# First head's keys loaded in pairs, an elementwise maximum of score tiles, and that head's softmax placed after the next head's first key tile, in a decode kernel of cached attention and a gated MLP

## The chip, the cores and the metric

The kernel runs on one core of one Trainium2 chip. The metric is device microseconds of one execution. The median of three runs is given, and one more execution is profiled.

## The reference

One token goes through two branches, which a scalar gate mixes. Cut to what matters:

```python
g = sigmoid((x * gate_w).sum(-1, keepdims=True))
# branch A: 32 query heads share 4 key/value heads, 65536 cached positions, 128 wide
q = (x @ wq).reshape(1, 1, 32, 128).transpose(0, 2, 1, 3)
k = repeat(k_cache, 8, axis=1);  v = repeat(v_cache, 8, axis=1)
p = softmax(einsum('bhqd,bhkd->bhqk', q, k) * 128 ** -0.5, axis=-1)
a = einsum('bhqk,bhkd->bhqd', p, v).reshape(1, 1, 4096) @ wo
# branch B: gelu(x @ w_in), its second half normalised, scaled by w_sp and
# shifted by b_sp, times its first half, then @ w_out
out = g * a + (1 - g) * b
```

All inputs are bfloat16. The caches of keys and of values are 64 MB each (4 heads of 16 MB), and with the weights about 162 MB are read.

## The kernel before, in words

**Tiles.** The cache of one key/value head (G = 4 heads) is cut into NT = 4 tiles of 4 MB. Partition p of a tile holds 128 consecutive positions of 128 bf16, 32 KB. `load_kv` (L189) loads one tile, or two neighbouring ones as one DMA of 8 MB, in which each partition's row is 64 KB. All loads, the weights too, go into one buffer `kv` with NKV = 5 places of 4 MB. The argument `at` says at which place a load begins. A load is issued by SyncE (L184, the queue SP), in program order, and first waits until whatever last read those places is done. Only the two results and some small vectors take another queue.

**A key tile**, `k_tile` (L398). In four steps of a quarter tile each, VectorE transposes in place (L403), and TensorE multiplies the result with the query matrix `wt` (L410, 8 matmuls per step), all of it accumulating into the PSUM tile `s_ps` (two buffers, tag "s"). ScalarE then copies it to a bf16 tile `sc` of 128 x 1024 (L421). The maximum of `sc` along the row is written to one column of `mx` by a reduction (L405); it is kept in the list `late` and issued in the next key tile, behind that tile's first transpose.

**A head's softmax**, `stats` (L424). It issues the reduction that is left (L425), reduces the four columns to one (`m1`, L427), and takes the maximum over the partitions by a transpose on TensorE (`mt_ps`, L429), a small reduction (`gm`), a copy (`gr`), a small matmul (`nb_ps`, L436) and a scaling (`nb`, L439). Then for each of the four tiles ScalarE computes the exponential with its sum (L443) and VectorE transposes the result into `pt` (L446). The first exponential is preceded by a load of ScalarE's function table.

**A value tile**, `v_tile` (L449), is 32 matmuls with `pt` as weights (L456), accumulating a head's four tiles in `o_ps`. `head_out` (L464) turns them into the head's part of the output vector, and `build_w` (L386) makes the query matrix `wt` of a head on VectorE. `project` (L503) multiplies a vector with rows of an output weight.

**The order.** Every engine executes in program order (a dependency between each two instructions of an engine is added at the end). The program first loads w_in to places 3 to 4.75 and wq to places 0 to 2, and computes branch B's vector and the queries. Head 0's keys follow as four loads of one tile each, to places 2, 3, 0 and 1, each followed by its `k_tile`. Then w_out is loaded to place 4 and projected, and `stats(0)` runs. For each further head g, in two halves h: a pair of its keys is loaded to places 2 and 3 (h = 0) or 3 and 4 (h = 1), the tile in place 3 is processed first and then the other, a pair of the values of head g-1 is loaded to places 0 and 1, and its two tiles are processed; in the second half `stats(g)` stands between the two value tiles. After the loop come the last head's values, wo and the output.

Of the kernel before, what the change touches and what calls it, by code (L numbers as in the profile page):

```python
# [8 lines left out]
FP32 = mybir.dt.float32  # L9
BF16 = mybir.dt.bfloat16  # L10
I32 = mybir.dt.int32
ACT = mybir.ActivationFunctionType
ALU = mybir.AluOpType
AX = mybir.AxisListType

P = 128
CT = 128
NKV = 5
B = 32
NB = P // B  # L20
VC = 4
CC = CT // VC
# [7 lines left out]
def kernel(  # L30
# [15 lines left out]
    nc = tc.nc  # L46
# [12 lines left out]
    NT = S // (P * CT)  # L59
# [9 lines left out]
    wk = ctx.enter_context(tc.tile_pool(name="wk", bufs=2))  # L69
    big = ctx.enter_context(tc.tile_pool(name="big", bufs=1))  # L70
# [9 lines left out]
    def same_weights(ins):  # L80
        held.add(ins.ins.name)
# [95 lines left out]
    def load(src, shape, at):  # L177
        n = 1
        for s in shape:
            n *= s  # L180
        v = kv[:, int(at * CT * P):int(at * CT * P) + n]
        if len(shape) == 2:
            v = v.rearrange("p (a b) -> p a b", b=shape[1])
        ins = nc.sync.dma_start(out=v, in_=src)  # L184
        if not first_load:
            first_load.append(ins.ins.name)
        return v

    def load_kv(src, g, j, at, n=1):  # L189
        h, i = divmod(j, 2)  # L190
        rows = src[0, g, 2 * h * CT * P:2 * (h + 1) * CT * P, :].rearrange(
            "(p c) d -> p (c d)", c=2 * CT)
        v = load(rows[:, i * CT * DH:(i + n) * CT * DH], (n * CT * DH,), at)
        return [v[:, i * CT * DH:(i + 1) * CT * DH] for i in range(n)]
# [60 lines left out]
    for t in range(2):  # L255
        nc.vector.tensor_tensor(  # L256
            out=xm[:, t], in0=xb_ps[:, t * P:(t + 1) * P].rearrange("p (i c) -> p c i", c=KC),
            in1=sel_i[:].unsqueeze(1).to_broadcast([P, KC, P // KC]), op=ALU.mult)
# [51 lines left out]
    for hf in range(2):  # L310
        nc.vector.tensor_tensor(
            out=zm[:, hf], in0=z_ps[:, hf * HN:hf * HN + ZN].rearrange("p (j c) -> p j c", c=FC),
            in1=own_b[:].unsqueeze(2).to_broadcast([P, B, FC]), op=ALU.mult)
    z = wk.tile([P, 2 * FC], FP32, name="z")
    nc.vector.tensor_reduce(out=z[:].rearrange("p (h c) -> p h c", h=2),
                            in_=zm.rearrange("p h j c -> p h c j"), axis=AX.X, op=ALU.add)
# [24 lines left out]
                            op=ALU.subtract)  # L341
# [19 lines left out]
    for k in range(NHB):  # L361
        xs = slice(k * NX // NHB, (k + 1) * NX // NHB)
        nc.vector.tensor_tensor(  # L363
            out=qm[:, xs], in0=q_ps[:, k * HN:(k + 1) * HN].rearrange("p (x j e) -> p x j e",
                                                                   j=B, e=2),
            in1=own_b[:].unsqueeze(1).unsqueeze(3).to_broadcast([P, NX // NHB, B, 2]), op=ALU.mult)
    q1 = wk.tile([P, NX, 2], FP32, name="q1")
    nc.vector.tensor_reduce(out=q1[:], in_=qm.rearrange("p x j e -> p x e j"), axis=AX.X,
                            op=ALU.add)
    q4 = wk.tile([P, NB, NX * 2], BF16, name="q4")  # L370
    nc.vector.tensor_tensor(
        out=q4[:], in0=q1[:].rearrange("p x e -> p (x e)").unsqueeze(1).to_broadcast(
            [P, NB, NX * 2]),
        in1=own_n[:].unsqueeze(2).to_broadcast([P, NB, NX * 2]), op=ALU.mult)
# [6 lines left out]
    for g in range(G):  # L381
        k, t0 = g * T2 // NB, g * T2 % NB
        nc.vector.tensor_copy(out=qs[:, g].rearrange("p b (t h) -> p b t h", t=T2),
                              in_=qv[:, k, t0:t0 + T2].rearrange("p t h b -> p b t h"))

    def build_w(g):  # L386
        for v in range(VC):
            nc.vector.tensor_tensor(
                out=wt[g % 2][:, v, :, :, v, :],
                in0=qs[:, g].unsqueeze(2).to_broadcast([P, BP, NB, REP]),  # L390
                in1=own_n[:].unsqueeze(1).unsqueeze(3).to_broadcast([P, BP, NB, REP]),
                op=ALU.mult)

    oa = const.tile([P, OC], BF16, name="oa")
    late = []
    sct, ptt, mxs, lss, o_ps = {}, {}, {}, {}, {}

    def k_tile(g, j, kn):  # L398
        kb = kn.bitcast(I32)
        n = CC * DH // 2  # L400
        s_ps = pss.tile([P, 2 * HN], FP32, name="s_ps", tag="s")
        for v in range(VC):
            nc.vector.transpose(out=kb[:, v * n:(v + 1) * n], in_=kb[:, v * n:(v + 1) * n])  # L403
            while late:
                nc.vector.reduce_max(**late.pop())  # L405
            kx = kn[:, v * CC * DH:(v + 1) * CC * DH].rearrange(
                "p (c h k e) -> p h e c k", h=2, k=B, e=2)
            for b in range(BP):
                for k in range(2):
                    ins = nc.tensor.matmul(  # L410
                        s_ps[:, k * HN:(k + 1) * HN],
                        lhsT=wt[g % 2][:, v, b].rearrange("p a v h -> p (a v h)"),
                        rhs=kx[:, b // 2, b % 2, k * CC // 2:(k + 1) * CC // 2, :],
                        start=(v == 0 and b == 0), stop=(v == VC - 1 and b == BP - 1),
                        skip_group_check=True)
                    if k > 0:
                        same_weights(ins)
        if g not in mxs:
            mxs[g] = wk.tile([P, NT], FP32, name="mx")
        sct[g, j] = scp.tile([P, CC * B], BF16, name="sc")  # L420
        nc.scalar.copy(out=sct[g, j][:], in_=s_ps[:])  # L421
        late.append(dict(out=mxs[g][:, j:j + 1], in_=sct[g, j][:], axis=AX.X))

    def stats(g):  # L424
        nc.vector.reduce_max(**late.pop())  # L425
        m1 = wk.tile([P, 1], FP32, name="m1")
        nc.vector.reduce_max(out=m1[:], in_=mxs[g][:], axis=AX.X)  # L427
        mt_ps = psm.tile([1, P], FP32, name="mt_ps", tag="m")
        nc.tensor.transpose(mt_ps[:], m1[:], ident_f[:])  # L429
        gm = wk.tile([1, REP], FP32, name="gm")  # L430
        nc.vector.tensor_reduce(out=gm[:], in_=mt_ps[:].rearrange("p (a h) -> p h a", h=REP),
                                axis=AX.X, op=ALU.max)
        gr = wk.tile([1, P // REP, REP], FP32, name="gr")
        nc.vector.tensor_copy(out=gr[:], in_=gm[:].unsqueeze(1).to_broadcast([1, P // REP, REP]))
        nb_ps = psm.tile([P, 1], FP32, name="nb_ps", tag="m")
        nc.tensor.matmul(nb_ps[:], lhsT=gr[:].rearrange("p a h -> p (a h)"),  # L436
                         rhs=ones_f[0:1, 0:1], start=True, stop=True)
        nb = wk.tile([P, 1], FP32, name="nb")
        nc.vector.tensor_scalar(out=nb[:], in0=nb_ps[:], scalar1=-SCALE, scalar2=None,  # L439
                                op0=ALU.mult)  # L440
        lss[g] = wk.tile([P, NT], FP32, name="ls")
        for j in range(NT):
            nc.scalar.activation(out=sct[g, j][:], in_=sct[g, j][:], func=ACT.Exp, scale=SCALE,  # L443
                                 bias=nb[:, 0:1], accum_out=lss[g][:, j:j + 1])
            ptt[g, j] = ptp.tile([P, CC, B], BF16, name="pt")
            nc.vector.transpose(out=ptt[g, j][:].rearrange("p c x -> p (c x)"),  # L446
                                in_=sct[g, j][:])
# [55 lines left out]
    def project(w, n, vec, c0, first=False, last=False):  # L503
        for c in range(n):
            for t in range(NB):
                nc.tensor.matmul(  # L506
                    out_ps[t * B:(t + 1) * B, :],
                    lhsT=vec[:, c0 + c:c0 + c + 1].to_broadcast([P, B]),
                    rhs=w[:, c, t * NO:(t + 1) * NO],
                    start=(first and c == 0), stop=(last and c == n - 1),  # L510
                    skip_group_check=True)


    build_w(0)
    for j, n, at in ((0, 1, 2), (1, 1, 3), (2, 1, 0), (3, 1, 1)):
        for i, kn in enumerate(load_kv(A_k_cache, 0, j, at, n)):
            k_tile(0, j + i, kn)
        if j == 1:
            build_w(1)
    project(load(B_w_out.rearrange("(p c) n -> p c n", c=FC), (FC, D), 4), FC, uT, 0, first=True)  # L520
    stats(0)
    for g in range(1, G):
        for h in range(2):
            kn = load_kv(A_k_cache, g, 2 * h, 2 + h, 2)
            for i in ((1, 0), (0, 1))[h]:
                k_tile(g, 2 * h + i, kn[i])
            if h == 0 and g + 1 < G:
                build_w(g + 1)
            vn = load_kv(A_v_cache, g - 1, 2 * h, 0, 2)
            v_tile(g - 1, 2 * h, vn[0])  # L530
            if h == 1:
                stats(g)
            v_tile(g - 1, 2 * h + 1, vn[1])
        head_out(g - 1)
# [61 lines left out]
```

## Time and profile before

| | |
|---|---|
| median of 3 runs | 382.27 us (382.05 to 382.38) |
| the profiled execution | 382.16 us, its span 380.7 us |
| busy | PE 233.2 us (61%), PEld 56.0 (15%), DVE 218.5 (57%), ACT 39.6 (10%), POOL 4.4 (1%) |
| DMA | 162.17 MB, mean 426 GB/s over the span |
| key transposes (L403) | 64, mean 2281 ns |
| score matmuls (L410) | 512, busy 141.8 us |
| value matmuls (L456) | 512, busy 61.7 us |
| maxima (L405, L425) | 16 reductions, mean 1210 and 1220 ns |
| exponentials (L443) | 16, mean 1137 ns |

PE is TensorE, PEld its weight loads, DVE VectorE, ACT ScalarE, POOL GpSimd and SP SyncE. Times in views are microseconds from the start of the span. A letter q behind an engine means its instruction queue. In a timeline a line holds the start, the length, the engine, the line of the kernel, the operation, the tile written and the tiles read, the shapes, the count, and in brackets the idle time of the engine before it and what ended that. The slices of the page cut the span into 40 equal parts; a digit is the busy share in tenths, 9 standing for 90% or more. The chain of waits follows the work that ended last back to what released it.

### The profile page before, as it was taken

How to read it: one execution, taken by the hardware profiler on the slowest of the kernel's cores; microseconds unless marked ns; L12 is line 12 of the kernel's file. 1: busy time of each engine (PE TensorE's matmuls, PEld its weight loads, DVE VectorE, ACT ScalarE, POOL GpSimd, SP SyncE). 2: the span in 40 equal slices, each digit the busy share in tenths (PEclk: the TensorE clock that was granted, in tenths of full speed). 3: DMA queues.
4: the chain of work that ended last, by engine and by line, in shares of the span. 5: the costliest groups of instructions: out<-in, count | busy, mean ns of one | idle time of the engine just before them, and what ended most of it. 6: DMA issues, size and time to landing. Idle time of an engine off the chain costs nothing.

```text
span 380.7 us, 2605 instructions
## 1 busy us (share of the span) xinstructions
PE 233.2 (61%) x1395; PEld 56.0 (15%) x800; DVE 218.5 (57%) x211; ACT 39.6 (10%) x55; POOL 4.4 (1%) x10
## 2 busy tenths in 40 slices
PE   0060657876157944796397729871977196839386
PEld 0010101111101210111011101120211011202113
DVE  4133288997597506966977059669970388460040
ACT  1001001110601100114010001050100000500000
POOL 4000000000000000000000000000000000000000
PEclk9995769899759895989688958895989579969789
DMA  9998999999999999999999999999999999999995
GB/s 386 496 420 379 411 438 441 437 483 430 387 420 441 441 436 441 427 441 441 434 436 441 441 427 434 406 423 441 434 434 429 420 441 442 436 410 430 424 443 223
DMA packets 3943, 162.17 MB, mean 426 GB/s; under 512 B 472, under 2 KB 476, under 8 KB 860
## 3 DMA queue, kind: packets, MB, share of 16 engines
q1 hardware_dynamic: 3892, 162.01, 98.8%
q8 instruction: 8, 0.13, 0.1%
q14 instruction: 3, 0.02, 0.0%
q10 hardware_dynamic: 40, 0.01, 0.0%
HBM read 162.01 MB, written 0.00 MB: 426 GB/s over the span
## 4 chain that ended last, share of the span: by engine, by line
DMA 57%; PE 26%; DVE 13%; ACT 2%; issue 1%; SPq 1%; DVEq 0%; ACTq 0%
DMA kv<-in_A_k_cache_dram 43%; PE s_ps L410 21%; DMA kv<-in_A_wo_dram 7%; DVE kv L403 7%; DMA kv<-in_A_v_cache_dram 7%; PE o_ps L456 4%; DVE pt L446 2%; DVE o_sb L470 1%; DVE mx L405 1%; ACT sc L421 1%; ACT sc L443 1%; DVE rowt L466 1%; SPq L184 1%; PE om_ps L476 0%; DVE osum L486 0%
## 5 line engine op out<-in xcount | busy, mean ns | idle before, releaser
L410 PE MATMUL s_ps<-kv,wt 128*128 128x512 bf16 x512 | 141.8, 437 | 80.2 <-DVE kv L403 80.2
L403 DVE STREAM_TRANSPOSE kv<-kv 128x2048 int32<-128x2048 int32 x64 | 142.7, 2281 | 54.3 <-DMA kv<-in_A_k_cache_dram 54.3
L456 PE MATMUL o_ps<-kv,pt 128*64 128x512 bf16 x512 | 61.7, 400 | 7.6 <-DMA kv<-in_A_v_cache_dram 7.6
L410 PEld LDWEIGHTS <-wt 128*128 128x128 bf16 x256 | 27.6, 108 | 195.6 <-issue 138.5
L421 ACT CAST sc<-s_ps 128x1024 bf16<-128x1024 f32 x16 | 16.2, 1012 | 249.9 <-PE s_ps L410 249.9
L456 PEld LDWEIGHTS <-pt 128*64 128x64 bf16 x256 | 16.1, 115 | 50.6 <-issue 48.1
L446 DVE STREAM_TRANSPOSE pt<-sc 128x1024 bf16<-128x1024 bf16 x16 | 18.6, 1217 | 6.8 <-ACT sc L443 6.8
L405 DVE TENSOR_REDUCE mx<-sc 128x1 f32<-128x1024 bf16 x12 | 14.5, 1210 | 9.9 <-ACT sc L421 9.9
L443 ACT ACTIVATE sc<-sc,nb 128x1024 bf16<-128x1024 bf16 x16 | 18.2, 1137 | 12.3 <-DVE nb L439 12.2
L466 DVE TENSOR_TENSOR rowt<-o_ps,own 128x1024 f32<-128x1024 f32 x4 | 4.8, 1195 | 24.9 <-PE o_ps L456 24.9
L476 PE MATMUL om_ps<-o_sb,hsel 128*32 128x128 f32 x8 | 2.3, 386 | 18.3 <-DVE o_sb L470 18.3
L425 DVE TENSOR_REDUCE mx<-sc 128x1 f32<-128x1024 bf16 x4 | 4.9, 1220 | 13.6 <-ACT sc L421 13.6
L296 PE MATMUL q_ps<-kv,xT 128*32 128x512 bf16 x64 | 5.6, 527 | 7.2 <-DMA kv<-in_A_wq_dram 7.2
L252 PE MATMUL xb_ps<-xg,spread 8*128 8x256 bf16 x1 | 0.4, 366 | 13.2 <-DMA xg<-in_gate_w_dram 13.2
L470 DVE TENSOR_REDUCE o_sb<-rowt 128x128 f32<-128x1024 f32 x4 | 7.5, 1872 | 0.1
L363 DVE TENSOR_TENSOR rowt<-q_ps,own_b 128x512 f32<-128x512 f32 x2 | 1.3, 686 | 10.8 <-PE q_ps L296 10.8
L296 PE MATMUL z_ps<-kv,xT 128*32 128x448 bf16 x64 | 5.9, 560 | 0.0
L495 PE MATMUL busy_ps<-wt 128*128 128x512 bf16 x23 | 5.8, 381 | 0.1
L506 PE MATMUL out_ps<-kv,oa 128*32 128x256 bf16 x128 | 4.2, 274 | 2.0 <-DMA kv<-in_A_wo_dram 2.0
L256 DVE TENSOR_TENSOR xm<-xb_ps,sel_i 128x128 f32<-128x128 f32 x2 | 0.5, 287 | 8.0 <-PE xb_ps L252 8.0
L552 ACT CAST out_sb<-out_ps 128x256 bf16<-128x256 f32 x1 | 0.4, 372 | 45.1 <-PE out_ps L506 45.1
L296 PEld LDWEIGHTS <-xT 128*32 128x32 bf16 x64 | 2.6, 136 | 14.6 <-issue 14.6
(90 smaller groups left out, 59.3 us busy)
## 6 DMA issues: line engine op xcount, KB each, us to landing
kv<-in_A_k_cache_dram SPq DMA_DIRECT2D x4, 4096.0 KB, 35.4
kv<-in_A_v_cache_dram SPq DMA_DIRECT2D x2, 4096.0 KB, 26.0
kv<-in_B_w_in_dram SPq DMA_DIRECT2D x1, 7168.0 KB, 19.4
kv<-in_A_wo_dram SPq DMA_DIRECT2D x1, 6144.0 KB
kv<-in_B_w_out_dram SPq DMA_DIRECT2D x1, 3584.0 KB
kv<-in_A_wo_dram SPq DMA_DIRECT2D x1, 1024.0 KB
kv<-in_A_wo_dram SPq DMA_DIRECT2D x1, 512.0 KB
kv<-in_A_wo_dram SPq DMA_DIRECT2D x2, 256.0 KB, 28.2
```

The lines of the kernel that those rows point to most:

```text
L296: ins = nc.tensor.matmul(ps[t * B:(t + 1) * B, k * HN:k * HN + n], lhsT=xT[:, i * KH + c:i * KH + c + 1].to_broadcast([P, B]), rhs=w[:, c, ...
L403: nc.vector.transpose(out=kb[:, v * n:(v + 1) * n], in_=kb[:, v * n:(v + 1) * n])
L405: nc.vector.reduce_max(**late.pop())
L410: ins = nc.tensor.matmul(s_ps[:, k * HN:(k + 1) * HN], lhsT=wt[g % 2][:, v, b].rearrange("p a v h -> p (a v h)"), rhs=kx[:, b // 2, b % 2, ...
L421: nc.scalar.copy(out=sct[g, j][:], in_=s_ps[:])
L425: nc.vector.reduce_max(**late.pop())
L443: nc.scalar.activation(out=sct[g, j][:], in_=sct[g, j][:], func=ACT.Exp, scale=SCALE, bias=nb[:, 0:1], accum_out=lss[g][:, j:j + 1])
L446: nc.vector.transpose(out=ptt[g, j][:].rearrange("p c x -> p (c x)"), in_=sct[g, j][:])
L456: ins = nc.tensor.matmul(o_ps[g][hs, e, :], lhsT=ptt[g, j][:, 2 * u:2 * u + 2, :].rearrange("p c x -> p (c x)"), rhs=vx[:, 2 * u + e], sta ...
L466: nc.vector.tensor_tensor(out=om8, in0=o_ps[g][:].rearrange("p e (v d) -> p (e v) d", d=DH), in1=own_8[:].unsqueeze(2).to_broadcast([P, 2 ...
L470: nc.vector.tensor_reduce(out=o_sb[:], in_=om8.rearrange("p x d -> p d x"), axis=AX.X, op=ALU.add)
L495: ins = nc.tensor.matmul(ps[:, :HN], lhsT=w[:, :P], rhs=w[:, :HN], start=True, stop=True, skip_group_check=True)
```

## The change

Three things change. Head 0's keys are loaded as two pairs, tiles 0 and 1 to places 2 and 3 and tiles 2 and 3 to places 0 and 1, instead of four single tiles; `build_w(1)` stays behind the second tile. The maximum of a head's scores is no longer taken by a reduction per tile: the first `sc` tile is kept as it is, each later one is joined by an elementwise maximum over 128 x 1024 into one bf16 tile `mx`, and `stats` reduces that tile once along its rows. And `stats(0)` is called after the first key tile of head 1 instead of before it. The other heads' `stats` stay where they are.

```diff
+    mx = big.tile([P, CC * B], BF16, name="mx")
+
+    def running_max(g, sc):
+        if g in mxs:
+            nc.vector.tensor_tensor(out=mx[:], in0=mxs[g][:], in1=sc[:], op=ALU.max)
+            mxs[g] = mx
+        else:
+            mxs[g] = sc
+
     def k_tile(g, j, kn):
...
             while late:
-                nc.vector.reduce_max(**late.pop())
+                running_max(*late.pop())
...
-        if g not in mxs:
-            mxs[g] = wk.tile([P, NT], FP32, name="mx")
         sct[g, j] = scp.tile([P, CC * B], BF16, name="sc")
         nc.scalar.copy(out=sct[g, j][:], in_=s_ps[:])
-        late.append(dict(out=mxs[g][:, j:j + 1], in_=sct[g, j][:], axis=AX.X))
+        late.append((g, sct[g, j]))
 
     def stats(g):
-        nc.vector.reduce_max(**late.pop())
+        while late:
+            running_max(*late.pop())
         m1 = wk.tile([P, 1], FP32, name="m1")
         nc.vector.reduce_max(out=m1[:], in_=mxs[g][:], axis=AX.X)
...
     build_w(0)
-    for j, n, at in ((0, 1, 2), (1, 1, 3), (2, 1, 0), (3, 1, 1)):
-        for i, kn in enumerate(load_kv(A_k_cache, 0, j, at, n)):
+    for j, at in ((0, 2), (2, 0)):
+        for i, kn in enumerate(load_kv(A_k_cache, 0, j, at, 2)):
             k_tile(0, j + i, kn)
-        if j == 1:
+        if j == 0:
             build_w(1)
     project(load(B_w_out.rearrange("(p c) n -> p c n", c=FC), (FC, D), 4), FC, uT, 0, first=True)
-    stats(0)
     for g in range(1, G):
         for h in range(2):
             kn = load_kv(A_k_cache, g, 2 * h, 2 + h, 2)
             for i in ((1, 0), (0, 1))[h]:
                 k_tile(g, 2 * h + i, kn[i])
+                if g == 1 and (g - 1) not in lss:
+                    stats(g - 1)
```

## The prediction

> **What bounds the kernel now.** I read the page's slices and queue table first, then the chain of waits, then the timelines of the DMA-issuing queue, of TensorE and of VectorE around the first heads. The page:
>
> ```profile
> DMA  9998999999999999999999999999999999999995
> ...
> q1 hardware_dynamic: 3892, 162.01, 98.8%
> ...
> kv<-in_B_w_in_dram SPq DMA_DIRECT2D x1, 7168.0 KB, 19.4
> ```
>
> The DMA row is full in all but the last slice, and one queue's packets fill 98.8% of 16 engines' span. PE is busy 61%, DVE 57%. The packet records confirm it: from the first packet (about 1.5 us) to the last weight there is no hole. So the time is the bytes plus any moment when the queue runs dry, and an engine's saving is worth nothing unless it opens or closes such a moment. What decides is how early each load is issued, against when the loads before it have drained. The queue's timeline (start, length, what):
>
> ```profile
> 73.12 0.33 SPq L184 DMA_DIRECT2D kv<-in_A_k_cache_dram  x1
> 94.83 0.33 SPq L184 DMA_DIRECT2D kv<-in_A_v_cache_dram  x1
> 119.04 0.33 SPq L184 DMA_DIRECT2D kv<-in_A_k_cache_dram  x1
> 137.69 0.33 SPq L184 DMA_DIRECT2D kv<-in_A_v_cache_dram  x1
> ```
>
> Call these K1a, V0a, K1b and V0b (8 MB each, two tiles). The chain of waits dates the landings of K1a and K1b at the ends of these pieces:
>
> ```profile
> 73.12 33.87 DMA kv<-in_A_k_cache_dram
> ...
> 119.04 26.66 DMA kv<-in_A_k_cache_dram
> ```
>
> That is 106.99 and 145.71. Between them V0a and K1b moved, so a pair takes 38.72 / 2 = 19.36 us, and gapless V0b would land at 145.71 + 19.36 = 165.07. What a load into an empty queue costs shows once: the 7168 KB of w_in (7.34 MB) landed 19.4 us after issue; at a pair's rate (8.39 MB in 19.36) its bytes take 16.9, so **2.5 us** are start, ramp and landing. V0b is gapless if issued by 165.07 - 19.36 - 2.5 = 143.2. It was issued at 137.69: a slack of 5.5 us.
>
> V0b overwrites V0a's place, so it waits for the last of V0a's matmuls (L456), which stand behind both of K1a's tiles on TensorE. I call these tile A (first) and tile B. TensorE:
>
> ```profile
> 109.43 11.32 PE L410 MATMUL s_ps<-kv,wt 128*128 128x512 bf16 x40 [10.76 <-DVE kv L403]
> 123.59 7.04 PE L410 MATMUL s_ps<-kv,wt 128*128 128x512 bf16 x24 [2.84 <-DVE kv L403]
> 130.56 7.10 PE L456 MATMUL o_ps<-kv,pt 128*64 128x512 bf16 x64
> ```
>
> The first row is tile A's 32 matmuls, ended at 119.03, and 8 of tile B; tile B ends at 130.6, V0a at 137.66. VectorE, with ScalarE's table load, shows the first head's softmax where it is now, in the idle time before K1a lands at 106.99:
>
> ```profile
> 97.13 0.16 DVE L427 TENSOR_REDUCE m<-mx 128x1 f32<-128x4 f32 x1
> 97.65 0.28 DVE L431 TENSOR_REDUCE gm<-mt_ps 1x8 f32<-1x128 f32 x1 [0.36 <-PE mt_ps L429]
> ...
> 101.52 4.64 DVE L446 STREAM_TRANSPOSE pt<-sc 128x1024 bf16<-128x1024 bf16 x4 [2.65 <-ACT sc L443]
> 107.02 11.09 DVE L403 STREAM_TRANSPOSE kv<-kv 128x2048 int32<-128x2048 int32 x5 [0.85 <-DMA kv<-in_A_k_cache_dram]
> ```
>
> ```profile
> 98.95 1.28 ACT L443 ACT_TABLE_LOAD   x1 [3.11 <-DVE nb L439]
> ```
>
> From the PE transpose of the maximum (97.34) to the last transposed weight (106.16) it takes 8.8 us, and DVE only hands over and transposes in that time.
>
> **What the Trainium skill says.** "VectorE: DVE Perf Modes", section on the perf-mode tier table: tensor_tensor on bf16 in SBUF runs at twice the single rate (1224 ns for 2048 elements), tensor_reduce at the single rate only. The trace agrees on the reduce (1.21 us for 1024); it has no large bf16 tensor_tensor. "ScalarE: Activation LUTs", section on what ACT_TABLE_LOAD costs: about 1283 ns, then a drain of 1380 ns. The trace agrees on the first (1.28), and shows no drain: the first Exp starts at 100.25, 1.30 after the load began. "TensorE: Matmul & The Clock Gate", Part 1: the array falls to half clock after idle windows of about 3.4 us and recovers after about as long of work. The trace agrees: windows of 4 us grant 0.50 from 104 to 112 and 1.00 from 116.
>
> **The change part by part.**
>
> *K of head 0 in pairs.* The bytes are the same, two issues fewer. Packets become 64 KB instead of 32 KB; the records give 2.422 us for one against 2 x 1.216, so 10 ns saved, times 256 / 16 per engine: -0.16 us. The first pair now also covers place 3, so its issue waits for w_in's matmuls (about 26), where wq is still flowing until about 39: hidden. Compute starts at K01's landing (59.77) instead of K00's (49.97). Then, at 8.89 us per four transposes: tile 0 to 68.7, tile 1 to 77.5, build_w(1) 0.9 to 78.4, TensorE done near 80. K1a needs those places: issued at 80 instead of 73.12, needed by 106.99 - 19.36 - 2.5 = 85.1: hidden, with 5 us left. The second pair lands near 79.2; tiles 2 and 3, with one elementwise maximum each and a 0.7 us wait for the ScalarE copy, end on DVE at 99.1, on TensorE at 101. V0a is issued then instead of 94.83, needed by 106.99 - 2.5 = 104.5 at the latest and 102.8 for the engines that drain first: hidden, narrowly.
>
> *The maximum.* Removed: 16 reductions of 1.21 and four of 0.16. Added: 12 tensor_tensor and four reductions of 1.21. Price of one, an estimate from that section: at the single rate it gives 2293 ns for 2048 elements, so the doubled rate saves 1069 ns by halving the elements' time; 1024 elements at the doubled rate are half of 1069 under 1224, or 0.69 us. Bounds: 0.6, and 1.22 if it is no faster than the reduce. I take 0.69. DVE saves about 2 us per head, off the path. In later heads the last maximum plus the reduce are 0.7 us longer than now, in front of mt_ps, which waits for V matmuls until 172.87 when m1 is ready at 171.86: hidden within 0.3. On tile A one maximum falls behind its first transpose; TensorE at half clock is the slower there, so tile A still ends at about 119.0 (bounds 118.5 and 119.6).
>
> *The softmax of head 0, moved.* It leaves DVE's idle stretch (now 99 to 107) and stands on the in-order engines between tiles A and B. Everything it issues moves: on DVE a reduce, four small ones and four transposes; on TensorE the transpose and two small matmuls; on ScalarE the table load and four Exps; no DMA. Queued behind it: tile B's transposes, B's matmuls, V0a's 64 matmuls, and SP waits for those with V0b. K1b's issue needs only tile A's place and w_out's, so it stays near 119, needed by 145.71 - 19.36 - 2.5 = 123.9: no loss. Steps: tile A ends on TensorE 119.03; softmax +8.8 = 127.85 (DVE's reduce of 1.2 fits before 119, ScalarE's copy of tile A fits before the bias is ready); tile B from its first transpose to its last matmul +12.0, as for tile A (107.02 to 119.03) and the first tiles after an idle stretch in heads 2 and 3 (12.1, 12.1, 12.4, and once 10.9), since TensorE has again idled over 9 us: 139.85; V0a's matmuls +7.1 = **146.95** (now 137.66). V0b's issue slips 9.3 where the slack is 5.5.
>
> *Sum.* V0b lands at 146.95 + 2.5 + 19.36 = 168.8 against 165.07: +3.7 by the last engine. But at that point the 16 engines are spread: most run dry at 143.9, a few at 145.4 to 145.7, each having served a 16 KB instruction packet. With the first packet at 146.95 + 1.4 (as from 0 to 1.5 at the start), most lose 4.5, plus up to 0.6 of ramp, and which engine ends last is decided by later such packets: up to +5.1. I take +4.3. All later loads then have as much more slack, so nothing is added or regained. 4.3 - 0.16 = **+4.1**. The profiled execution took 382.16 (span 380.7, 1.5 around it), 0.03% under the median of 382.27: 382.16 + 4.1 = 386.3.
>
> **Rivals.**
>
> 1. *Cover holds (not slower).* Mechanism: V0b's issue, price the slip, deciding point 143.2. If the block between A and B costs under 5.5 us instead of 9.3, no hole opens. For it: from mt_ps to the last transpose head 1 took only 7.5, having its table, and tile B from a warm array is 10.9; both together still leave a slip of 6.9. Against: the order per engine is fixed by the program, and no DVE work of tile B can overtake the transposes that wait for Exp. Only a much shorter chain, or B running ahead of the softmax (the change not acting as its words say), gives this: 382.0.
> 2. *A second hole.* V0a's issue at 101 has under 2 us of margin. If head 0's pairs run later (maxima at 1.22, half clock in tile 2), it reaches 103 to 104 and adds 0.5 to 2 us: 387 to 388.5.
> 3. *A real gain*, from head-level DVE relief: against it the DMA row without holes, and only 0.16 us to get. About 381.
>
> **How the numbers follow.** Hole at V0b 0.82, rival 1 0.08, rival 2 0.08, rival 3 0.02. A measurement here can tell about 0.2% (0.76 us) from no change. Low end: tile A at 118.5, softmax 8.8, tile B 10.9, V0b at 145.3, cost by the last engine 2.1 less 0.16: 384.1. High end: 5.1, another 0.5 from slower maxima, part of rival 2: 388.0. Slower 0.90, same 0.08, faster 0.02.
>
> **What would show it.** Right: V0b's issue near 147 with L456 as its releaser; a slice near 145 where DMA and GB/s fall by some 4 us' worth; K1b still issued near 119 and landing near 145.6; every later issue with more slack and the same spacing; 12 tensor_tensor rows near 0.69 us. Wrong in part: V0a issued after 104, or K1a's landing past 107. Wrong altogether: DMA full through 140 to 150, or V0b issued before 143.

## The result and the profile after

The changed kernel takes **385.9 us** (median of 6 runs, 385.04 to 386.88) against 382.22 us (6 runs, 382.05 to 382.38): 3.7 us slower, ratio 1.0096, 95% interval 1.0081 to 1.0112. The forecast was 386.3. The profiled execution's span is 384.3 us, 3.6 above the 380.7 of before.

The GB/s row of the page of before, and then the slices of the page of the changed kernel, whose DMA row is to be held against the full one of before:

```profile
GB/s 386 496 420 379 411 438 441 437 483 430 387 420 441 441 436 441 427 441 441 434 436 441 441 427 434 406 423 441 434 434 429 420 441 442 436 410 430 424 443 223
```

```profile
DMA  9999999999999988999999999999999999999995
GB/s 382 491 437 437 425 424 430 391 454 437 438 430 437 430 350 327 437 437 437 437 431 437 437 437 437 431 437 430 437 437 431 437 430 410 431 399 426 450 414 236
...
q1 hardware_dynamic: 3604, 162.01, 97.9%
```

The same 162.01 MB, but the 15th and 16th slices (about 134 to 154 us) moved 350 and 327 GB/s where before they moved 436 and 441. A slice is 9.6 us: (86 + 114) x 9.6 / 441 = 4.4 us' worth of transfer is missing there. No pair of slices away from there lost half as much.

The issuing queue's timeline of the changed kernel (start, length, what), with K1a, V0a, K1b, V0b and the next load:

```profile
79.08 0.33 SPq L184 DMA_DIRECT2D kv<-in_A_k_cache_dram  x1
100.66 0.33 SPq L184 DMA_DIRECT2D kv<-in_A_v_cache_dram  x1
118.43 0.33 SPq L184 DMA_DIRECT2D kv<-in_A_k_cache_dram  x1
145.79 0.33 SPq L184 DMA_DIRECT2D kv<-in_A_v_cache_dram  x1
156.82 0.33 SPq L184 DMA_DIRECT2D kv<-in_A_k_cache_dram  x1
```

V0b went from 137.69 to 145.79; the loads on either side of it hardly moved. What was ahead of V0b, first on VectorE, then on TensorE:

```profile
109.55 6.69 DVE L412 STREAM_TRANSPOSE kv<-kv 128x2048 int32<-128x2048 int32 x3
116.16 1.18 DVE L435 TENSOR_REDUCE m<-mx 128x1 f32<-128x1024 bf16 x1
...
122.42 4.64 DVE L454 STREAM_TRANSPOSE pt<-sc 128x1024 bf16<-128x1024 bf16 x4 [2.65 <-ACT sc L451]
126.98 8.85 DVE L412 STREAM_TRANSPOSE kv<-kv 128x2048 int32<-128x2048 int32 x4
```

```profile
109.16 9.24 PE L419 MATMUL s_ps<-kv,wt 128*128 128x512 bf16 x32 [6.89 <-DVE kv L412]
118.24 0.27 PE L437 MATMUL mt_ps<-ident_f,m 128*1 128x128 f32 x1
119.22 0.35 PE L444 MATMUL nb_ps<-ones_f,gr 1*128 1x1 f32 x2 [0.71 <-DVE gr L442]
129.31 9.42 PE L419 MATMUL s_ps<-kv,wt 128*128 128x512 bf16 x32 [9.74 <-DVE kv L412]
138.66 7.10 PE L464 MATMUL o_ps<-kv,pt 128*64 128x512 bf16 x64
```

Tile A is the first matmul row, tile B the fourth. Between them TensorE sits 9.74 us idle, waiting for tile B's first transpose, which stands behind the softmax. V0a's matmuls end at 145.76, and 0.03 later V0b is issued.

The records of the single packets complete it. The 16 engines ran dry between 143.1 and 144.9. They got V0b's first packets at 146.74 to 147.32, the first of them 0.95 us after the start of the issue. Averaged over the 16, they stood empty for 3.3 us around that place (before: not at all). And these first 64 KB packets took 2.9 to 3.4 us, where the median is 2.42.

### The profile page after: what moved, and what is told of

Same layout as the page of the kernel before. It is cut to its first block, busy times and chain, and to the rows that moved or that the text cites. A ratio compares the mean times of both kernels' runs of the same rounds, so it can differ in the third digit from the quotient of the medians.

```text
span 384.3 us, 2602 instructions
## 1 busy us (share of the span) xinstructions
PE 222.9 (58%) x1397; PEld 54.5 (14%) x800; DVE 211.2 (55%) x207; ACT 39.6 (10%) x55; POOL 4.4 (1%) x10
## 3 DMA queue, kind: packets, MB, share of 16 engines
q1 hardware_dynamic: 3604, 162.01, 97.9%
HBM read 162.01 MB, written 0.00 MB: 422 GB/s over the span
## 4 chain that ended last, share of the span: by engine, by line
DMA 71%; PE 17%; DVE 9%; issue 1%; SPq 0%; ACTq 0%; ACT 0%; DVEq 0%
DMA kv<-in_A_k_cache_dram 53%; PE s_ps L419 13%; DVE kv L412 9%; DMA kv<-in_A_wo_dram 7%; DMA kv<-in_A_v_cache_dram 7%; DMA wb<-in_B_b_sp_dram 5%; PE o_ps L464 3%; PE z_ps L296 1%; SPq L184 0%; PE small_ps L271 0%; ACTq L198 0%; DVE mx L402 0%; ACT out_sb L561 0%; PE out_ps L514 0%; ACTq L199 0%
## 5 line engine op out<-in xcount | busy, mean ns | idle before, releaser
L419 PE MATMUL s_ps<-kv,wt 128*128 128x512 bf16 x512 | 132.2, 411 | 92.4 <-DVE kv L412 92.3
L412 DVE STREAM_TRANSPOSE kv<-kv 128x2048 int32<-128x2048 int32 x64 | 142.4, 2279 | 75.7 <-DMA kv<-in_A_k_cache_dram 75.7
L419 PEld LDWEIGHTS <-wt 128*128 128x128 bf16 x256 | 26.2, 102 | 199.2 <-issue 116.5
L402 DVE TENSOR_TENSOR mx<-mx,sc 128x1024 bf16<-128x1024 bf16 x8 | 5.5, 687 | 12.7 <-ACT sc L428 12.7
L435 DVE TENSOR_REDUCE m<-mx 128x1 f32<-128x1024 bf16 x4 | 4.8, 1210 | 0.1
```

The lines of the kernel that those rows point to most:

```text
L402: nc.vector.tensor_tensor(out=mx[:], in0=mxs[g][:], in1=sc[:], op=ALU.max)
L419: ins = nc.tensor.matmul(s_ps[:, k * HN:(k + 1) * HN], lhsT=wt[g % 2][:, v, b].rearrange("p a v h -> p (a v h)"), rhs=kx[:, b // 2, b % 2, ...
```

## The experiments

All are single edits of one of the two kernels or of an earlier experiment. "Empty" is the time, averaged over the 16 engines and read from the packet records, in which they had no packet around the late load or loads. "Over" is the median less that of the kernel before on the same chip. The issues and the empty time come from the profiled execution, whose time can differ from the median: it was 0.8 us below it for "changed, softmax back" and 1.0 below it for "pairs only". The table is ordered by V0b's issue, and those that are late at K1b stand last; each run is told below.

| kernel | K1b issued | V0b issued | empty, us | over, us |
|---|---|---|---|---|
| maximum only | 119.05 | 133.69 | 0 | -0.2 |
| before | 119.04 | 137.69 | 0 | 0 |
| softmax after B, V0b split | 118.64 | 138.70 | 0 | -0.4 |
| six extra transposes | 118.75 | 142.46 | 0.2 | 1.6 |
| softmax after B | 119.14 | 142.66 | 0.5 | 1.5 |
| changed, V0b split | 118.98 | 143.11 | 0.8 | 1.2 |
| changed, table loaded early | 118.31 | 144.40 | 1.9 | 2.6 |
| **changed** | 118.43 | 145.79 | 3.3 | 3.7 |
| softmax moved only | 119.18 | 146.78 | 4.0 | 4.7 |
| ten extra transposes | 117.99 | 147.66 | 4.9 | 5.4 |
| changed, softmax back, table early | 122.58 | 137.72 | 0.5 | 1.6 |
| changed, softmax back | 124.19 | 139.22 | 1.2 | 1.9 |
| pairs only | 126.72 | 145.37 | 2.2 | 5.7 |

**Softmax put back.** `stats(0)` returns to its old place in the changed kernel:

```diff
     project(load(B_w_out.rearrange("(p c) n -> p c n", c=FC), (FC, D), 4), FC, uT, 0, first=True)
+    stats(0)
...
-                if g == 1 and (g - 1) not in lss:
-                    stats(g - 1)
```

> The changed kernel with the first head's softmax put back before the loop (pairs and elementwise maximum stay). Theory 'hole' (the moved softmax makes V0b's issue late, and the queue runs dry): tile A now starts after the softmax, near 109.6 instead of 106.75, since VectorE ends head 0's tiles at 98.7 and the softmax takes 8.8 from the transpose of the maximum at about 100.8; tile B ends near 131, V0b is issued near 138 to 139, before the 142 to 143 at which it starts to cost; no hole, 382.0 to 382.3. Rival 'late pairs' (head 0's later start, 59.4 instead of 50.0, is what delays V0b): the loss stays, 385 to 386.

Measured 384.08 us, ratio 1.0047 (1.0032 to 1.0062). V0b was early, as the hole theory has it, but half of the loss stayed. Its issuing queue shows where:

```profile
100.80 0.33 SPq L184 DMA_DIRECT2D kv<-in_A_v_cache_dram  x1
124.19 0.33 SPq L184 DMA_DIRECT2D kv<-in_A_k_cache_dram  x1
139.22 0.33 SPq L184 DMA_DIRECT2D kv<-in_A_v_cache_dram  x1
```

K1b is at 124.19 instead of 118.43. It waits for tile A, and with head 0's tiles done later, the softmax before the loop reaches past K1a's landing: the first key transposes of head 1 start at 112.6. So there are **two deadlines**, K1b's and V0b's, and the old place of the softmax misses the first when the keys come in pairs. My expectation put tile A at 109.6; it overlooked that the last elementwise maximum waits 3.0 us for ScalarE's copy.

**Only the move**, in the kernel before, with single loads and reductions:

```diff
     def stats(g):
-        nc.vector.reduce_max(**late.pop())
+        if g > 0:
+            nc.vector.reduce_max(**late.pop())
...
-    stats(0)
...
                 k_tile(g, 2 * h + i, kn[i])
+                if g == 1 and (g - 1) not in lss:
+                    stats(g - 1)
```

> The kernel before with one part of the change alone: the first head's softmax after the first key tile of head 1 (its last reduction is already issued within that tile, so that it doesn't wait for the next head's copy). Single loads and the reductions per tile stay. Theory 'hole': the same block stands between tiles A and B, and tile B has one reduction of 1.2 us more inside; V0b issued near 146 to 147, a hole of 3 to 4 us, 385.5 to 387. Rival 'late pairs': without pairs head 0 is early as before, and the time is 382.2.

Measured 386.80 us, ratio 1.0121 (1.0104 to 1.0138). The move alone makes the hole at V0b, larger than the whole change does; the pairs are not needed for it.

**V0b in two loads**, in the changed kernel:

```diff
-            vn = load_kv(A_v_cache, g - 1, 2 * h, 0, 2)
+            if g == 1 and h == 1:
+                vn = [load_kv(A_v_cache, 0, 2 + i, i, 1)[0] for i in range(2)]
+            else:
+                vn = load_kv(A_v_cache, g - 1, 2 * h, 0, 2)
```

> The changed kernel with one load made two: the second half of head 0's values (V0b) is loaded as two tiles, each to its own place, so that the first waits only for the first of V0a's tiles. Theory 'hole': that tile's matmuls end 3.5 us earlier, near 142.2, and the first load is issued then; at the point where lateness starts to cost (142.1, as 145.79 cost 3.7), so the hole closes to under 0.5 us: 382.2 to 382.7. A theory in which VectorE or TensorE work itself is longer by the change (no relation to V0b's issue) expects 385.9 as before.

Measured 383.38 us, ratio 1.0032 (1.0019 to 1.0046), above the expected range. Only one load was changed, in what it waits for and in the size of its packets (32 KB instead of 64), and 2.5 of the 3.7 us went. What is left goes with a first issue at 143.11 instead of 142.2, 0.8 us of empty engines, and first packets of mostly 1.6 to 2.0 us where 32 KB otherwise take 1.22.

**The table loaded early**, in the changed kernel:

```diff
+    early = wk.tile([P, 1], FP32, name="early")
+    nc.scalar.activation(out=early[:], in_=stat[:, 5:6], func=ACT.Exp)
     build_w(0)
```

> The changed kernel with a one-column Exp on ScalarE added before head 0's tiles, so that the function table is loaded in idle time and not inside the moved softmax. Theory 'hole': the softmax is shorter by the load's 1.28 us, V0b is issued near 144.5, and each microsecond counts fully: 384.6. Rival (the loss is a fixed cost of a restart of the queue, or lies elsewhere): 385.9.

Measured 384.73 us, ratio 1.0068 (1.0053 to 1.0083), 1.1 to 1.2 us less than the changed kernel. V0b was issued 1.39 us earlier: the hole shrinks by what the chain in front of it shrinks. That excludes a fixed cost as the main part.

**Extra work and nothing else.** In the kernel before, scratch transposes stand between tile A and tile B:

```diff
+    extra = big.tile([P, CC * B], BF16, name="extra")
+    nc.gpsimd.memset(extra[:], 0.0)
     build_w(0)
...
                 k_tile(g, 2 * h + i, kn[i])
+                if g == 1 and h == 0 and i == 1:
+                    for _ in range(6):      # or 10
+                        nc.vector.transpose(out=extra[:], in_=extra[:])
```

> The kernel before, with nothing of the change, and six added VectorE transposes of a scratch tile (128x1024 bf16, 1.16 us each) between tile A and tile B of head 1. VectorE then is done with them at 115.8 + 7.0 = 122.8, tile B's transposes and its one reduction take 10.1, TensorE 1.9 more: tile B ends at 134.8 instead of 130.6 and V0b is issued at 141.9. Theory 'hole' (engines lose about the issue less 142.4, as the runs so far give: 143.11 lost 0.85, 144.40 lost 1.93, 145.79 lost 3.39): inside the slack, no loss, 382.0 to 382.5. Rival 'added VectorE work counts' (no threshold): 7 us of it show in part, 384 or more.

Measured 383.91 us, ratio 1.0040 (1.0025 to 1.0054): the expectation failed. V0b was issued at 142.46, 0.6 later than worked out (a scratch transpose takes 1.27 us, not 1.16), with only 0.2 us of empty engines, and still 1.6 us were lost.

> The same with ten transposes: VectorE done at 127.4, tile B ends near 139.5 to 140, V0b issued at 146.6 to 147. Theory 'hole': 4.2 to 4.6 us of empty queue and some 0.4 to 0.6 for the restart, 386.5 to 387.5. Rival 'no threshold': only two thirds more than with six.

Measured 387.69 us, ratio 1.0141 (1.0126 to 1.0156), slightly above what was expected, with V0b at 147.66. From six to ten transposes the issue slips 5.2 us and the time grows 3.8.

**The softmax after tile B**, one tile later still:

```diff
-    scp = ctx.enter_context(tc.tile_pool(name="scp", bufs=NT + 1))
-    ptp = ctx.enter_context(tc.tile_pool(name="ptp", bufs=NT + 2))
+    scp = ctx.enter_context(tc.tile_pool(name="scp", bufs=NT + 2))
+    ptp = ctx.enter_context(tc.tile_pool(name="ptp", bufs=NT + 1))
...
-        while late:
+        while late and late[-1][0] == g:
             running_max(*late.pop())
...
-                if g == 1 and (g - 1) not in lss:
-                    stats(g - 1)
+            if g == 1 and h == 0:
+                stats(0)
```

> The changed kernel with the first head's softmax one key tile later still: behind tile B, ahead of V0a's matmuls (one score tile more is kept, and one weight tile less, so that it fits). Theory 'two deadlines' (K1b must be issued by about 123, which only tile A decides, V0b by 142.4, which tile B, the softmax and V0a's matmuls decide): K1b stays at 118.4; tile B starts at 116.2 and ends on TensorE near 127; the transpose of the maximum follows at about 127.3, the first weights are there 5.4 later and V0a's matmuls run into the transposes of the others: V0b issued near 140, inside. No hole, 382.0 to 382.5. Rival (any move past the loop's start costs, or the pairs do by themselves): 384 or more.

Measured 383.79 us (382.74 to 384.39 over 12 runs), ratio 1.0038 (1.0028 to 1.0048). The expectation failed: K1b was in time, but V0b was issued at 142.66, not 140. TensorE of this kernel:

```profile
127.25 0.27 PE L437 MATMUL mt_ps<-ident_f,m 128*1 128x128 f32 x1
128.23 0.35 PE L444 MATMUL nb_ps<-ones_f,gr 1*128 1x1 f32 x2 [0.71 <-DVE gr L442]
132.72 9.89 PE L464 MATMUL o_ps<-kv,pt 128*64 128x512 bf16 x64 [4.15 <-DVE pt L454]
```

The first weights came when expected, and V0a's matmuls started at 132.72; but they took 9.89 us instead of 7.10. The weights are not what held them up: the last of the four was ready at 136.06, with 6.5 us of matmuls still to come. The granted clock was 0.50 from 132 to 138, after TensorE's 4.15 us of idle time, where in the changed kernel V0a's matmuls ran at 1.00 throughout. At 7.10 us they would have ended at 139.8, as expected, so the clock accounts for the whole miss; a version that keeps it up there was not tried. As with six transposes, an issue just past the point costs over 1 us.

**The pairs alone**, in the kernel before:

```diff
-    for j, n, at in ((0, 1, 2), (1, 1, 3), (2, 1, 0), (3, 1, 1)):
-        for i, kn in enumerate(load_kv(A_k_cache, 0, j, at, n)):
+    for j, at in ((0, 2), (2, 0)):
+        for i, kn in enumerate(load_kv(A_k_cache, 0, j, at, 2)):
             k_tile(0, j + i, kn)
-        if j == 1:
+        if j == 0:
```

> The kernel before with the pairs alone: reductions per tile and the softmax before the loop stay. In the kernel with pairs and elementwise maximum but the softmax put back, K1b was issued at 124.19 and lost 1.05 us. Here VectorE has one reduction more in each tile of head 0 and waits for the copy in tile 1: head 0's tiles end near 102.4, V0a is issued near 104.3, the softmax ends near 115.6, tile A near 127.6, so K1b is issued near 127.7. Theory 'two deadlines': a hole of 4 to 5 us at K1b and perhaps 1 at V0a, 386.5 to 388. Rival (the pairs are free, since their packets are larger and the bytes the same): 382.0.

Measured 387.95 us (386.95 to 388.9), ratio 1.0148 (1.0127 to 1.0168), with V0a issued at 104.57 (0.7 us of empty engines) and K1b at 126.72 (1.5): two restarts, and the dearest of all versions.

**Softmax after tile B, and V0b split** as above. This is the version in which both deadlines should be met:

> The kernel with the softmax behind tile B (issue of V0b at 142.66, 0.5 us of empty queue, and first packets of 3.1 to 3.4 us instead of 2.42), with V0b loaded as two tiles in addition, as in the run that split it in the changed kernel. The first tile now waits only for V0a's first 32 matmuls, which end near 136.4, so the queue has 6 us of margin at V0b and K1b is issued at 119. Theory 'two deadlines, plus a slow first packet when one is missed': nothing is lost, 382.0 to 382.3, as before; the larger packets of the pairs and the smaller ones of the split change it by less than 0.2. Rival (the pairs cost something by themselves beside these holes): 383 or more.

Measured 381.87 us (381.73 to 382.32 over 13 runs), ratio 0.9992, interval 0.9984 to 1.0000, 0.1 below the expected range. Its issuing queue:

```profile
118.64 0.33 SPq L184 DMA_DIRECT2D kv<-in_A_k_cache_dram  x1
138.70 3.78 SPq L184 DMA_DIRECT2D kv<-in_A_v_cache_dram  x2
```

The first half of V0b is issued at 138.70, and the loss is gone, with pairs, elementwise maximum and a moved softmax all in place. It is the fastest of all medians here, but its interval reaches 1, so a gain over the kernel before is not shown.

**The maximum alone**, in the kernel before, with the `running_max` of the change:

```diff
             while late:
-                nc.vector.reduce_max(**late.pop())
+                running_max(*late.pop())
...
-        late.append(dict(out=mxs[g][:, j:j + 1], in_=sct[g, j][:], axis=AX.X))
+        late.append((g, sct[g, j]))
...
     def stats(g):
-        nc.vector.reduce_max(**late.pop())
+        while late:
+            running_max(*late.pop())
```

> The kernel before with the elementwise maximum alone: single loads, the softmax before the loop. VectorE works some 2 us less per head. Theory 'only deadlines count': all deadlines were met before, so nothing changes: 382.1 to 382.4. Rival (VectorE's relief shows): 381.5 or less.

Measured 382.01 us, ratio 0.9994 (0.9986 to 1.0002), 0.1 below the expected range. V0b is issued 4 us earlier (133.69), and the time can't be told apart from no change: work taken from an engine off the bound bought only slack here.

**Softmax put back, table early**, in the changed kernel:

```diff
+    early = wk.tile([P, 1], FP32, name="early")
+    nc.scalar.activation(out=early[:], in_=stat[:, 5:6], func=ACT.Exp)
     build_w(0)
...
+    stats(0)
...
-                if g == 1 and (g - 1) not in lss:
-                    stats(g - 1)
```

> The kernel with pairs, elementwise maximum and the softmax put back, which issued K1b at 124.19 and lost 1.9 us in the median, with the early Exp in addition, so that the softmax is 1.28 us shorter. Theory 'two deadlines': tile A begins 1.3 us earlier and K1b is issued near 122.9, at the edge: most of the loss goes, 382.1 to 383.2. Rival (the pairs lose it elsewhere): 384.1 as without it.

Measured 383.84 us, ratio 1.0037 (1.0024 to 1.0051), above the range. K1b was issued at 122.58, even a little earlier than expected, and yet only a fraction of the 1.9 us went, if any: the intervals of the two versions overlap. So the edge is not sharp, as with six transposes.

## Why the prediction was right

*The bound and the mechanism* held. The queue runs dry once, at V0b, and splitting that one load gave back most of the loss. Every other load of the changed kernel was in time: K1a at 79.08 (worked out: 80), V0a at 100.66 (101), K1b at 118.43 (119). The cover that the prediction named for the pairs, 5 us at K1a and under 2 at V0a, was enough: no engine stood empty at either.

*The terms of the slip.* The softmax's chain, from the transpose of the maximum at 118.24 to the last weight at 127.06, took 8.8 us, as before. Tile B took 11.8 from its first transpose to its last matmul (12.0), V0a's matmuls 7.10 (7.1). Tile A ended 0.6 earlier than the 119.03 carried over. Together V0b slipped by 8.1 instead of 9.3. The elementwise maximum took 0.65 to 0.69 us, from these rows of the changed kernel grouped by shape, against the estimate of 0.69:

```profile
L402 DVE TENSOR_TENSOR mx<-mx,sc 128x1024 bf16<-128x1024 bf16 x8 | 5.5, 687 | 12.7 <-ACT sc L428 12.7
L402 DVE TENSOR_TENSOR mx<-sc 128x1024 bf16<-128x1024 bf16 x4 | 2.6, 650 | 0.0
```

*The price of the hole.* Worked out as 4.5 us for most engines plus up to 0.6 of ramp, of which 4.3 was taken. With the slip 1.2 shorter, 3.3 us of empty engines came, and slower first packets of about 0.7 on top (about 3.1 against 2.42): 4.0, less 0.16 for the larger packets, where the span grew by 3.6. The slip, 1.2 too long, is the term that was off most; the ramp, which the 4.3 left out, took about 0.7. The two errors have opposite signs, so that the forecast came within 0.4 us is in part luck.

*A reading that was off.* The prediction has the engines run dry at 143.9 and a first packet 1.4 us after its issue, from 1.5 at the start of the program. The packet records of the kernel before show the last packets of K1b ending between 143.3 and 143.8 on twelve engines and up to 145.2 on the others; 143.9 is when the landings are signalled, 0.4 to 0.5 later. They show the program's first packet at 1.0, and in nine runs with a late load its first packet came 0.95 to 0.97 us after the issue. Both readings are late by about the same, so the 4.5 us between them stand.

*The sharpness.* The prediction allowed 143.2 as the last free moment, which it counted back from the landing on the last engine. The runs show that it is earlier: 138.70 costs nothing, 142.46 already 1.6 us. Counted for the engines that run dry first, at 143.3, less 0.95, it is about 142.4, an estimate from these packets. Rival 1 is out, since it needed an issue before 143; even that would not have been enough. Rival 2 (a second hole at V0a) did not happen here, but is what the pairs alone do. Rival 3 found no support: VectorE's relief alone gave 0.9994.

*What the prediction did not see* is why the three parts belong together. With pairs, the softmax before the loop misses K1b's deadline (1.9 us with the elementwise maximum, 5.7 in all with the reductions and a late V0a). The new place frees K1b and misses V0b's by more.

*Still open.* Near the edge (six transposes, the softmax back with an early table) the time grew by 1.6 us where empty engines and slow packets account for about 0.7 in the one and 1.2 in the other. The engines also finished less evenly at the end, by 1.1 and 0.6 us averaged over the 16; what spreads them wasn't tried. The versions with pairs that miss a deadline also vary more from run to run (385.04 to 386.88 for the change) than those without pairs (387.54 to 387.8 with ten transposes).

## What to carry to other kernels

Where one queue of loads is full from end to end, write down for each load what releases its place and when the queue before it drains. A piece of work may move freely as long as no load's issue comes near that deadline, and a microsecond beyond it cost about a microsecond here, with a restart on top. A move that keeps one deadline can break the next one: here the softmax stood in front of K1b at its old place and in front of V0b at its new one, and a place behind both tiles, with V0b split so that its first half waits for half as much, kept both.

## What was not expected of the hardware

The drained queue did not come back at full speed. In every run that restarted it after a clear hole, the first packets came 0.95 us after the issue and most of the first 64 KB packets took 2.8 to 3.5 us instead of 2.42. With six extra transposes V0b was issued at 142.46 and its first packets came at 143.41, where in the kernel before the engines had gone over to it between 143.3 and 145.2. They stood empty for only 0.2 us on average, yet eleven of the 16 had a first packet of 2.7 to 3.4 us.

ScalarE's table load sat behind the wait for the bias of the first Exp (it began at 119.85, 0.1 after the bias was ready), in the changed kernel as before. A one-column Exp in an idle stretch took it off the chain, and V0b's issue came 1.39 us earlier.

With the softmax after tile B, TensorE waited 4.15 us for the first weights, and for V0a's matmuls behind that wait the granted clock was 0.50 until 138. They took 2.8 us longer than in the changed kernel, which is what made V0b's issue late.
